# Sorting each partition's keys with 61 alternate-block stages at 30 falling distances in place of 69 stages of pruned odd-even merges

## The chip, the cores and the metric

The kernel runs on one core of a Trainium2 chip. The metric is the device time of one execution in microseconds (us). Before the change it was measured three times: 2129.62, 2132.74 and 2145.99 us; the median is 2132.74 us.

The engines are called as the profile calls them: PE is TensorE, DVE is VectorE, ACT is ScalarE, POOL is GpSimd and SP is SyncE, which issues most DMAs. Each engine works through its own queue of instructions in order; semaphores hold an instruction until what it reads or overwrites is ready.

## The reference

A GraphSAGE layer with mean aggregation: for each of 800,000 edges the row of the source node is added to the row of the destination node, the sums are scaled, and two 64x64 products are added.

```
N, deg, D = 12500, 64, 64
E = N * deg
def reference(x, src, dst, deg_inv, w_self, w_neigh):
    N = x.shape[0]
    # mean-aggregate neighbor features onto each destination node
    nsum = _segment_sum(x[src], dst, N)
    h_neigh = nsum * deg_inv[:, None]
    # GraphSAGE: W * CONCAT(h_v, AGG(h_u)) == W_self h_v + W_neigh h_N(v)
    return x @ w_self + h_neigh @ w_neigh
```

`src` and `dst` are drawn at random, `x` is 12,500 x 64 in 32-bit floats.

## The kernel before

The kernel sorts the edges by buckets of 144 destinations by 128 sources, so that gather and scatter become matrix products with one-hot matrices. It has these steps, one behind the other:

- **Keys** (`make_keys`, L405 to L414). The 800,000 edges lie as 128 partitions of 6,250. ACT and DVE make one 32-bit key of each edge, in seven pieces of columns, into buffer `a`.
- **Sorting each partition** (`sort_runs`, L221). Every partition's 6,250 keys are sorted along the columns by compare-exchange stages, all partitions at once. A stage reads one of the buffers `a` and `b` and writes the other. For a distance `dist` and a set `v` of columns, `emit` writes the minimum of columns `i` and `i + dist` to `i`, and the maximum to `i + dist`: two DVE instructions for each group of regular spacing (L232). Columns that a stage doesn't compare, but that the next one needs in the other buffer, are copied by ACT (L235). `spans` turns a set of columns into runs of equal length and spacing, so that one instruction takes many runs; `128x390x8` below is 390 runs of 8 columns.
- **Preparation** (`prepare`, `self_terms`, L515 to L599). It has nothing to do with the keys: `x` is split into two 16-bit floats and the product with `w_self` is made. The scheduler lays it beside the first stages of the sort. It has six ACT operations over 128x6272 elements (L538, L563, L565, L568, L573, L574), two such on DVE (L540, L564), and 26 small ACT copies from and to PE (L592, L597).
- **Finding rows** (`find_rows`, L443 to L466). ACT (L454) and DVE (L456) count, for each of 256 buckets of rows, how many keys lie below a bound in a window of the sorted columns. PE turns the counts, and POOL gathers runs of keys by them (L473).
- **Merging, decoding and sums.** DVE merges the gathered runs (L284, L296, L313, L328), the keys are decoded, and then PE multiplies one-hot matrices with `x` and sums into destinations (L827, L883), with ACT and DVE beside it.

The sort before is an odd-even merge sort. Thirteen levels merge ever finer interleaved sequences, and each level has a first stage at half its spacing and then stages at falling odd multiples; ranges that random keys hardly reach are pruned. That makes 69 stages, on average 3,012 compared pairs each. All spacings are powers of two. Where a level begins, ACT copies its untouched columns in one go (`alone`, `again`).

The last level is cut in two at column 2,560 (`SPLIT`): `below` runs all its stages for the low columns, then `above` for the rest, and the counts of the first 54 buckets (`EARLY`), which lie in the low columns, are laid on ACT beside `above`. `after_sort` writes this order out by hand, and everything from there to the end of the kernel; the stages ahead of it are placed by the scheduler, together with the preparation.

At the very end the kernel counts the edges that it found, and runs `general`, a slow loop over all edges, if the count isn't 800,000.

Of the kernel before, what the change touches and what calls it, by code (L numbers as in the profile page):

```python
# [17 lines left out]
AF = mybir.ActivationFunctionType  # L18
# [34 lines left out]
EARLY = 54  # L53
SHARED = 100
SPLIT = 2560
SIGMA = 6.0
LOWER = 2240
CLOSE = 32
# [92 lines left out]
def view(t, off, dims):  # L151
    a = t[:, :]
    dims = [d for d in dims if d[1] != 1] or [[1, 1]]
    return bass.AP(tensor=a.tensor, offset=a.offset + off, ap=[a.ap[0]] + dims)


def reach(k, n, total=None):

    i = np.arange(max(n - k, 0))
    m = 2.0 * i + k + 1
    var = m * (total - m) / total if total else m
    i = i[(k + 1.0) ** 2 <= SIGMA ** 2 * var]
    return (int(i[0]), int(i[-1]) + 1) if len(i) else (0, 0)


def distances(n, total=None):

    out = []  # L170
    k = 1
    while k < n:
        lo, hi = reach(k, n, total)
        if hi > lo:
            out.insert(0, (k, lo if lo > 3 else 0, hi))
        k *= 2
    return out


def spans(at):  # L180

    if not len(at):
        return []
    cut = np.flatnonzero(np.diff(at) != 1)
    out = []
    for lo, hi in zip(at[np.r_[0, cut + 1]].tolist(), (at[np.r_[cut, len(at) - 1]] + 1).tolist()):
        s = out[-1] if out else None
        if s and s[2] == hi - lo and (s[1] == 1 or lo - (s[0] + (s[1] - 1) * s[3]) == s[3]):
            if s[1] == 1:
                s[3] = lo - s[0]  # L190
            s[1] += 1
        else:
            out.append([lo, 1, hi - lo, 0])
    return out


def sort_levels(n):

    out = []
    R = 1
    while R < n:
        R *= 2
    at = np.arange(n)
    while R > 1:
        h = R // 2
        stages = [(h, at[(at % R < h) & (at + h < n)])]
        for k, lo, hi in distances(-(-n // R), -(-n // h)):
            i = at // R  # L210
            stages.append((k * R - h, at[(at % R >= h) & (i >= lo) & (i < hi) & (at + k * R - h < n)]))
        sets = [set(v.tolist()) | set((v + d).tolist()) for d, v in stages]
        assert all(x <= y for x, y in zip(sets[1:], sets[2:]))
        alone = sorted(set(range(n)) - sets[0])
        again = sorted(sets[0] - sets[1]) if len(sets) > 1 else []
        out.append((stages, np.array(alone, int), np.array(again, int)))
        R = h
    return out


def sort_runs(nc, bufs, n):  # L221

    levels = sort_levels(n)
    cur, oth = bufs

    def emit(src, dst, dist, v, low, cut, alone, again):
        for op, sh in ((OP.min, 0), (OP.max, dist)):
            for lo, g, l, st in spans(v[(v + sh >= low) & (v + sh < cut)]):  # L230
                x, y = (view(src, lo + o, [[st, g], [1, l]]) for o in (0, dist))
                nc.vector.tensor_tensor(view(dst, lo + sh, [[st, g], [1, l]]), x, y, op=op)  # L232
        for at, x, y in ((alone, src, dst), (again, dst, src)):
            for lo, g, l, st in spans(at[(at >= low) & (at < cut)]):
                nc.scalar.activation(view(y, lo, [[st, g], [1, l]]), view(x, lo, [[st, g], [1, l]]), AF.Copy)  # L235

    none = np.array([], int)
    for stages, alone, again in levels[:-1]:
        for j, (dist, v) in enumerate(stages):
            emit(cur, oth, dist, v, 0, n, *((none, none) if j else (alone, again)))  # L240
            cur, oth = oth, cur
    below, above = [], []
    stages, alone, again = levels[-1]
    edge = [SPLIT]
    for (first, _), (then, _) in zip(stages[-2::-1], stages[:0:-1]):
        edge.insert(0, edge[0] + max(first, then))
    assert edge[0] < n and not ((again > SPLIT) & (again < edge[0])).any()
    for j, (dist, v) in enumerate(stages):
        for l, low, cut in ((below, 0, edge[j]), (above, edge[j], n)):
            l.append(lambda a=(cur, oth, dist, v, low, cut, *((none, none) if j else (alone, again))): emit(*a))  # L250
        cur, oth = oth, cur
    return cur, below, above

# [86 lines left out]
class Kernel:  # L340
# [75 lines left out]
    def sort_edges(self, mps):  # L416

        nc, tc = self.nc, self.tc
        self.l1b = ExitStack()
        self.l1 = l1 = self.l1b.enter_context(tc.tile_pool(name="l1", bufs=1, side="right"))  # L420
        b = l1.tile([128, PITCH1], F32, name="b")
        self.c1 = l1.tile([128, 3, NC1], F32, name="c1")
        self.prow = l1.tile([128, 128], F32, name="prow")
        nc.gpsimd.iota(self.prow, pattern=[[PITCH1, 128]], base=0, channel_multiplier=0,
                       allow_small_or_imprecise_dtypes=True)
        self.l1ab = ExitStack()
        a = self.l1ab.enter_context(tc.tile_pool(name="l1a", bufs=1, side="right")).tile([128, PITCH1], F32, name="a")
        for t in (a, b):
            nc.gpsimd.memset(t[:, RUN:], BIG)
        with tc.tile_pool(name="raw", bufs=1) as raw:  # L430
            with tc.manual_schedule():
                self.make_keys(raw, a)
                nc.sync.dma_start(self.c1, self.I["c1"])
                for p in range(2):
                    nc.sync.dma_start(self.c2[p], self.I[f"c2_{p}"])
        self.runs, self.below, self.above = sort_runs(nc, (a, b), RUN)
        assert self.runs is b
        with tc.tile_pool(name="xp", bufs=1) as xp:
            self.prepare(xp, mps)
            self.self_terms(xp, mps)  # L440
        self.start = []
# [596 lines left out]
    def after_sort(self, es, mps, aps):  # L1038
# [5 lines left out]
        with tc.manual_schedule():  # L1044
            for step in self.below:
                step()
            tc.nc.sync.dma_start(self.d1[:, :SPLIT], self.runs[:, :SPLIT])
            rows = self.find_rows(0, mps)
            for i, step in enumerate(self.above):
                step()  # L1050
                while next(rows) + 1 < EARLY * (i + 1) // len(self.above):
                    pass
            tc.nc.sync.dma_start(self.d1[:, SPLIT:], self.runs[:, SPLIT:])
            self.l1ab.close()
# [125 lines left out]
```

## Time and profile before

| | |
|---|---|
| three runs | 2129.62, 2132.74, 2145.99 us |
| span of the profiled execution | 2141.8 us |
| DVE busy | 1998.3 us, 93% of the span |
| PE busy | 1022.8 us, 48% |
| ACT busy | 1260.8 us, 59% |
| keys begun, first sort stage begun | 3.63 us, 42.54 us |
| last sort stage ended | 512.46 us |
| first gather on POOL | 534.77 us |

The page of the profile gives the span alone for the profiled execution; it lies inside the range of the three runs and 9.1 us above their median. Up to 512 us the kernel is nearly one engine's work: DVE compares, ACT and PE work on the preparation in the first part, and POOL waits. From there to about 1,100 us DVE merges with POOL's gathers beside it. The rest, 1,042 us, is the matrix work, in which PE, ACT and DVE are all busy.

### The profile page before, as it was taken

The page shows a single profiled execution, that of the slowest core. Times are in us where ns is not written, and L with a number is a line of the kernel's source. Part 1 is how long each engine was busy: PE and PEld are TensorE (multiplying, and loading weights), DVE is VectorE, ACT ScalarE, POOL GpSimd, SP SyncE. Part 2 cuts the span into 40 slices and gives each one's busy share as a digit, 9 for nine tenths or more (in the row PEclk, how much of TensorE's full clock was granted, in tenths as well). Part 3 has the DMA queues.
Part 4 walks back from the last instruction along what each step waited for, and adds up shares of the span by engine and source line. Part 5 has one row for each costly group of instructions (what it writes and reads, how often), then busy time and mean ns, then how long its engine had stood idle before and what let it go on. Part 6 is the DMA issues. An engine that isn't in the chain of part 4 may idle for free.

```text
span 2141.8 us, 59532 instructions
## 1 busy us (share of the span) xinstructions
PE 1022.8 (48%) x26057; PEld 885.4 (41%) x26057; DVE 1998.3 (93%) x2172; ACT 1260.8 (59%) x1744; POOL 593.8 (28%) x867
## 2 busy tenths in 40 slices
PE   0140000000000000000299999999987799999997
PEld 0130000000000000000188788787876687888886
DVE  8999999999899999999999999999999988898887
ACT  7470000009700000162399999999998788888886
POOL 1000000000889888879810100000143000000000
PEclk9995555555555555555599999999999899999999
DMA  6040000000010000012477777777886677877874
GB/s 191 14 111 0 0 0 0 0 24 37 21 23 20 19 15 12 13 58 70 150 263 279 279 280 270 272 281 269 285 295 243 222 283 284 296 289 275 280 297 157
DMA packets 108220, 330.78 MB, mean 154 GB/s; under 512 B 53680, under 2 KB 61824, under 8 KB 107440
## 3 DMA queue, kind: packets, MB, share of 16 engines
q1 hardware_dynamic: 90784, 306.65, 39.4%
q0 software_dynamic: 14352, 18.65, 4.1%
q8 instruction: 205, 3.36, 0.6%
q10 hardware_dynamic: 2816, 1.61, 0.3%
q14 instruction: 63, 0.52, 0.1%
HBM read 307.86 MB, written 18.99 MB: 153 GB/s over the span
## 4 chain that ended last, share of the span: by engine, by line
PE 36%; DVE 30%; POOL 19%; issue 8%; ACT 5%; DMA 2%; ACTq 0%; DVEq 0%; POOLq 0%; SPq 0%
PE ct L827 21%; PE acc L883 14%; POOL u L473 13%; DVE a L232 10%; DVE b L232 10%; POOL pad L384 3%; ACT xg L837 2%; DVE ohd L802 2%; POOL v L633 2%; DVE ohs L799 2%; PE po L951 1%; DVE xg L835 1%; ACT junk L610 1%; DVE u L296 1%; ACT junka L454 1%
## 5 line engine op out<-in xcount | busy, mean ns | idle before, releaser
L837 ACT ACTIVATE xg<-ct 128x1024 f16<-128x1024 f32 (+1 forms) x991 | 934.8, 1105 | 102.2 <-PE ct L827 83.7
L827 PE MATMUL ct<-xh,ohs 128*128 128x128 f16 x8526 | 606.8, 223 | 47.7 <-issue 19.9
L827 PEld LDWEIGHTS <-ohs 128*128 128x128 f16 x8526 | 501.9, 99 | 91.7 <-issue 38.0
L473 POOL DMA_INDIRECT u<-d,ix x256 | 327.6, 1280 | 532.6 <-ACT junka L454 491.3
L296 DVE TENSOR_TENSOR u<-u 128x256 f32<-128x256 f32 (+47 forms) x494 | 452.6, 947 | 22.4 <-ACT u L280 15.3
L883 PE MATMUL acc<-ohd,xg 64*128 64x72 f16 x17052 | 413.0, 195 | 49.5 <-issue 27.1
L799 DVE TENSOR_SCALAR ohs<-slb,pidx 128x3584 f16<-128x3584 bf16 x305 | 351.0, 1151 | 32.8 <-PE ct L827 28.4
L883 PEld LDWEIGHTS <-xg 64*128 64x128 f16 x17052 | 327.1, 95 | 128.2 <-issue 47.4
L802 DVE TENSOR_TENSOR ohd<-iota,dlT 128x2016 f16<-128x2016 bf16 x305 | 366.7, 1202 | 0.0
L700 PE MATMUL tr<-idb,l 128*128 128x128 bf16 x68 | 9.1, 275 | 464.2 <-ACT l L694 460.6
L232 DVE TENSOR_TENSOR a<-b 128x106 f32<-128x106 f32 (+31 forms) x114 | 228.6, 2058 | 1.3
L232 DVE TENSOR_TENSOR b<-a 128x106 f32<-128x106 f32 (+36 forms) x112 | 227.4, 2081 | 1.0
L280 ACT ACTIVATE u<-u 128x256 f32<-128x256 f32 (+15 forms) x94 | 47.4, 595 | 281.6 <-DVE u L284 281.6
L463 PE MATMUL stp<-idf,st 128*128 128x128 f32 x2 | 0.9, 446 | 422.3 <-DVE st L461 422.3
L700 PEld LDWEIGHTS <-l 128*128 128x128 bf16 x68 | 5.5, 117 | 467.5 <-ACT l L694 464.0
L959 POOL DMA_DIRECT2D out<-o x24 | 22.8, 952 | 574.2 <-DVE o L958 491.2
L463 PEld LDWEIGHTS stp<-idf,st 128*128 128x128 f32 x2 | 0.4, 182 | 422.7 <-issue 422.7
L235 ACT ACTIVATE a<-b 128x106 f32<-128x106 f32 (+12 forms) x20 | 13.5, 709 | 214.1 <-DVE b L232 207.6
L835 DVE CAST xg<-ct 128x1024 f16<-128x1024 f32 x78 | 95.2, 1222 | 43.3 <-PE ct L827 43.2
L864 POOL DMA_INDIRECT lx<-xt,lxi x28 | 52.5, 1876 | 292.2 <-DVE lxi L862 165.9
L633 POOL DMA_INDIRECT v<-d,ix x68 | 89.9, 1323 | 63.5 <-ACT ix L663 44.6
L235 ACT ACTIVATE b<-a 128x1024 f32<-128x1024 f32 (+19 forms) x32 | 23.0, 771 | 130.4 <-DVE a L232 130.2
(135 smaller groups left out, 888.4 us busy)
## 6 DMA issues: line engine op xcount, KB each, us to landing
slb<-sl SPq DMA_DIRECT2D x305, 896.0 KB
u<-d,ix POOLq DMA_INDIRECT x256, 2.5
xt<-xh SPq DMA_DIRECT2D x1, 3136.0 KB
own<-os SPq DMA_DIRECT2D x12, 256.0 KB
fo<-own SPq DMA_DIRECT2D x24, 126.0 KB
out<-o POOLq DMA_DIRECT2D x24, 126.0 KB, 4.3
rd<-dst SPq DMA_DIRECT2D x4, 521.0 KB
rs<-src SPq DMA_DIRECT2D x4, 521.0 KB
```

The lines of the kernel that those rows point to most:

```text
L232: nc.vector.tensor_tensor(view(dst, lo + sh, [[st, g], [1, l]]), x, y, op=op)
L296: nc.vector.tensor_tensor(to, at(cur, ln + lo, n), at(cur, lo + k, n), op=op)
L384: self.nc.gpsimd.memset(self.pad, 0.0)
L473: nc.gpsimd.indirect_dma_start(out=u[:nr, p * w:(p + 1) * w], out_offset=None, in_=src, in_offset=bass.IndirectOffsetOnAxis(ap=self.start[ ...
L633: self.nc.gpsimd.indirect_dma_start(out=self.v[:, k].bitcast(F32), out_offset=None, in_=flat(self.d2[part], 128 * PITCH2[part]), in_offset ...
L799: nc.vector.tensor_scalar(s.rearrange("p c s -> p (c s)"), b, self.pidx[:, :1], None, op0=OP.is_equal)
L802: nc.vector.tensor_tensor(d, self.iota[:, None].to_broadcast([128, 14, HN, 2]), ix, op=OP.is_equal)
L827: nc.tensor.matmul(ct[:, i * 128:(i + 1) * 128], cols[i][0], self.xh[:, (b0 + i) % NB].rearrange("p a f -> p (a f)"), start=True, stop=True)
L835: nc.vector.tensor_copy(xg[:, :cnt * 128], ct[:, :cnt * 128])
L837: nc.scalar.activation(xg[:, :cnt * 128], ct[:, :cnt * 128], AF.Copy)
L864: nc.gpsimd.indirect_dma_start(out=x, out_offset=None, in_=self.xt, in_offset=bass.IndirectOffsetOnAxis(ap=ix.bitcast(U32), axis=0))
L883: nc.tensor.matmul(acc[h][:, db % OCT * HN:(db % OCT + 1) * HN], xg[r, i * 128:(i + 1) * 128], d[r], start=db % OCT == 0 and sb == 0, stop ...
```

## The change

The levels are replaced by a table of 61 stages, `GAPS`, of a distance and 0 or 1. At distance `g` the columns are cut into blocks of `g`; a stage with 0 compares block 0 with 1, 2 with 3 and so on, and a stage with 1 compares block 1 with 2, 3 with 4. There are 30 distances, from 2,568 down to 1, each used twice, and distance 1 a third time. A stage compares 2,944 pairs on average. What a stage leaves out at either end of the columns (`np.setdiff1d`) is copied by ACT in every stage. The last ten stages (`APART`, distances 5 to 1) are cut in two at column 2,560 as the last level was.

```diff
+APART = 10
+GAPS = ((2568, 0), (2568, 1), (1957, 0), (1957, 1), (1542, 0), (1542, 1), (1136, 0), (1136, 1), (867, 0), (867, 1), (659, 0), (659, 1), (509, 1), (509, 0), (393, 1), (393, 0), (319, 0), (319, 1), (245, 0), (245, 1), (186, 0), (186, 1), (145, 0), (145, 1), (114, 0), (114, 1), (88, 0), (88, 1), (68, 0), (68, 1), (53, 0), (53, 1), (41, 0), (41, 1), (31, 0), (31, 1), (24, 0), (24, 1), (18, 0), (18, 1), (14, 0), (14, 1), (11, 0), (11, 1), (9, 0), (9, 1), (7, 0), (7, 1), (6, 0), (6, 1), (5, 0), (5, 1), (4, 0), (4, 1), (3, 0), (3, 1), (2, 0), (2, 1), (1, 0), (1, 1), (1, 0))
...
-def sort_levels(n):
+def sort_stages(n):
...
+    every = np.arange(n)
+    for gap, odd in GAPS:
+        v = every[:n - gap]
+        v = v[v // gap % 2 == odd]
+        out.append((gap, v, np.setdiff1d(every, np.r_[v, v + gap])))
     return out
...
-        for at, x, y in ((alone, src, dst), (again, dst, src)):
-            for lo, g, l, st in spans(at[(at >= low) & (at < cut)]):
-                nc.scalar.activation(view(y, lo, [[st, g], [1, l]]), view(x, lo, [[st, g], [1, l]]), AF.Copy)
-
-    none = np.array([], int)
-    for stages, alone, again in levels[:-1]:
-        for j, (dist, v) in enumerate(stages):
-            emit(cur, oth, dist, v, 0, n, *((none, none) if j else (alone, again)))
-            cur, oth = oth, cur
+        for lo, g, l, st in spans(alone[(alone >= low) & (alone < cut)]):
+            nc.scalar.activation(view(dst, lo, [[st, g], [1, l]]), view(src, lo, [[st, g], [1, l]]), AF.Copy)
+
+    for dist, v, alone in stages[:-APART]:
+        emit(cur, oth, dist, v, 0, n, alone)
+        cur, oth = oth, cur
     below, above = [], []
-    stages, alone, again = levels[-1]
+    stages = stages[-APART:]
...
-    for j, (dist, v) in enumerate(stages):
+    for j, (dist, v, alone) in enumerate(stages):
         for l, low, cut in ((below, 0, edge[j]), (above, edge[j], n)):
-            l.append(lambda a=(cur, oth, dist, v, low, cut, *((none, none) if j else (alone, again))): emit(*a))
+            l.append(lambda a=(cur, oth, dist, v, low, cut, alone): emit(*a))
```

Counted from the two lists of stages: before, 226 DVE instructions with 415,716 columns (minima and maxima together) and 52 ACT copies with 34,300 columns; after, 198 DVE instructions with 359,200 columns and 87 ACT copies with 22,050. Behind the sort, the instructions of every engine are the same and stand in the same order; the lines of `kernel.py` behind the diff move up by 12.

Three places show how the instructions move. In the rows, `x2` at the end means two such instructions in a row, and the names are those of the tiles written and read.

The first place is DVE's queue where the last piece of keys is made and the sort begins (L410 to L414 make keys, L232 compares). Before:

```order
L410 SCALAR_TENSOR_TENSOR g<-h,rd 128x1040
L411 TENSOR_SCALAR a<-g 128x1040
L412 SCALAR_TENSOR_TENSOR g<-g,a 128x1040
L413 SCALAR_TENSOR_TENSOR s_226<-s_226,g 128x1040
L414 SCALAR_TENSOR_TENSOR a<-rs,s_226 128x1040
L232 TENSOR_TENSOR b<-a 128x2154 x2
L232 TENSOR_TENSOR a<-b 128x2048
```

The same place in DVE's queue after (L398 to L402 make keys, L223 compares):

```order
L398 SCALAR_TENSOR_TENSOR g<-h,rd 128x1040
L223 TENSOR_TENSOR b<-a 128x2568 x2
L399 TENSOR_SCALAR a<-g 128x1040
L400 SCALAR_TENSOR_TENSOR g<-g,a 128x1040
L401 SCALAR_TENSOR_TENSOR s_226<-s_226,g 128x1040
L402 SCALAR_TENSOR_TENSOR a<-rs,s_226 128x1040
L223 TENSOR_TENSOR a<-b 128x1114 x2
```

The first stage, which reads columns 0 to 5,135, now stands ahead of the last four key instructions, which make columns 5,210 to 6,249. The second stage stands right behind them, and reads columns 5,136 to 6,249 of `b`, which ACT copies.

The second place is ACT's queue in the preparation (L565 to L574 over 128x6272 elements, L592 and L597 small copies, L235 the sort's copies). Before:

```order
L565 ACTIVATE xh<-y 128x98x64
L592 ACTIVATE xs<-xt 128x512
L568 ACTIVATE y<-x,scl 128x6272
L597 ACTIVATE os<-pw 128x512
L592 ACTIVATE xs<-xt 128x512
L573 ACTIVATE z,s_530<-y 128x6272
L235 ACTIVATE a<-b 128x106
L597 ACTIVATE os<-pw 128x512
L592 ACTIVATE xs<-xt 128x512
L574 ACTIVATE z,s_531<-y,lim 128x6272
```

The same place in ACT's queue after (L553, L556, L561 and L562 are the four long operations, L225 the sort's copies):

```order
L553 ACTIVATE xh<-y 128x98x64
L585 ACTIVATE os<-pw 128x512
L580 ACTIVATE xs<-xt 128x512
L225 ACTIVATE a<-b 128x659
L556 ACTIVATE y<-x,scl 128x6272
L225 ACTIVATE b<-a 128x509
L585 ACTIVATE os<-pw 128x512
L225 ACTIVATE b<-a 128x367
L580 ACTIVATE xs<-xt 128x512
L225 ACTIVATE a<-b 128x142
L561 ACTIVATE z,s_517<-y 128x6272
L580 ACTIVATE xs<-xt 128x512
```

One copy of 106 columns stood among the four long operations; now the copies of stages 12, 13 and 14 stand between them (659; 509 and 367; 142 columns), and those of stage 15 (393 and 355) behind the fourth.

The third place is DVE's queue where short runs are compared. Before, at runs of 8:

```order
L232 TENSOR_TENSOR a<-b 128x390x8 x2
L232 TENSOR_TENSOR b<-a 128x247x8 x2
L232 TENSOR_TENSOR a<-b 128x359x8 x2
L232 TENSOR_TENSOR b<-a 128x375x8 x2
L232 TENSOR_TENSOR a<-b 128x383x8 x2
L232 TENSOR_TENSOR b<-a 128x387x8 x2
L232 TENSOR_TENSOR a<-b 128x389x8 x2
```

After, at distances 9 and 7:

```order
L223 TENSOR_TENSOR b<-a 128x347x9 x2
L223 TENSOR_TENSOR a<-b 128x346x9
L223 TENSOR_TENSOR a<-b 128x4
L223 TENSOR_TENSOR a<-b 128x346x9
L223 TENSOR_TENSOR a<-b 128x4
L223 TENSOR_TENSOR b<-a 128x446x7 x2
L223 TENSOR_TENSOR a<-b 128x445x7
L223 TENSOR_TENSOR a<-b 128x6
```

Eight stages at one spacing have become two, and runs of an odd length, every second of which begins at an odd column, take the place of runs of a power of two.

More of the change, by code (lines that the diff above doesn't have):

```diff
@@ L194, in spans, with emit @@
     return out
-def sort_levels(n):
+def sort_stages(n):
     out = []
[L202 to L217, printed above, removed]
+    every = np.arange(n)
[3 more added lines that the diff above has]
+        out.append((gap, v, np.setdiff1d(every, np.r_[v, v + gap])))
     return out
 def sort_runs(nc, bufs, n):
-    levels = sort_levels(n)
+    stages = sort_stages(n)
     cur, oth = bufs
-    def emit(src, dst, dist, v, low, cut, alone, again):
+    def emit(src, dst, dist, v, low, cut, alone):
         for op, sh in ((OP.min, 0), (OP.max, dist)):
@@ L232, in emit @@
                 nc.vector.tensor_tensor(view(dst, lo + sh, [[st, g], [1, l]]), x, y, op=op)
-        for at, x, y in ((alone, src, dst), (again, dst, src)):
-            for lo, g, l, st in spans(at[(at >= low) & (at < cut)]):
-                nc.scalar.activation(view(y, lo, [[st, g], [1, l]]), view(x, lo, [[st, g], [1, l]]), AF.Copy)
-    none = np.array([], int)
-    for stages, alone, again in levels[:-1]:
-        for j, (dist, v) in enumerate(stages):
-            emit(cur, oth, dist, v, 0, n, *((none, none) if j else (alone, again)))
-            cur, oth = oth, cur
+        for lo, g, l, st in spans(alone[(alone >= low) & (alone < cut)]):
[3 more added lines that the diff above has]
+        cur, oth = oth, cur
     below, above = [], []
-    stages, alone, again = levels[-1]
+    stages = stages[-APART:]
     edge = [SPLIT]
-    for (first, _), (then, _) in zip(stages[-2::-1], stages[:0:-1]):
+    for (first, *_), (then, *_) in zip(stages[-2::-1], stages[:0:-1]):
         edge.insert(0, edge[0] + max(first, then))
-    assert edge[0] < n and not ((again > SPLIT) & (again < edge[0])).any()
-    for j, (dist, v) in enumerate(stages):
+    assert edge[0] < n
+    for j, (dist, v, alone) in enumerate(stages):
         for l, low, cut in ((below, 0, edge[j]), (above, edge[j], n)):
-            l.append(lambda a=(cur, oth, dist, v, low, cut, *((none, none) if j else (alone, again))): emit(*a))
+            l.append(lambda a=(cur, oth, dist, v, low, cut, alone): emit(*a))
         cur, oth = oth, cur
```

## The prediction

> **What bounds the kernel now.** I read the page first: its span, the chain that ended last, and the groups of the sort.
>
> ```profile
> span 2141.8 us, 59532 instructions
> PE 36%; DVE 30%; POOL 19%; issue 8%; ACT 5%; DMA 2%; ACTq 0%; DVEq 0%; POOLq 0%; SPq 0%
> PE ct L827 21%; PE acc L883 14%; POOL u L473 13%; DVE a L232 10%; DVE b L232 10%; POOL pad L384 3%; ACT xg L837 2%; DVE ohd L802 2%; POOL v L633 2%; DVE ohs L799 2%; PE po L951 1%; DVE xg L835 1%; ACT junk L610 1%; DVE u L296 1%; ACT junka L454 1%
> L232 DVE TENSOR_TENSOR a<-b 128x106 f32<-128x106 f32 (+31 forms) x114 | 228.6, 2058 | 1.3
> L232 DVE TENSOR_TENSOR b<-a 128x106 f32<-128x106 f32 (+36 forms) x112 | 227.4, 2081 | 1.0
> L235 ACT ACTIVATE a<-b 128x106 f32<-128x106 f32 (+12 forms) x20 | 13.5, 709 | 214.1 <-DVE b L232 207.6
> L235 ACT ACTIVATE b<-a 128x1024 f32<-128x1024 f32 (+19 forms) x32 | 23.0, 771 | 130.4 <-DVE a L232 130.2
> ```
>
> The sort's compares (L232) are 226 instructions and 228.6 + 227.4 = 456.0 us of DVE, with 1.3 + 1.0 = 2.3 us of idle time before them, and 20% of the chain. ACT's copies (L235) take 36.5 us, and it is ACT that waits for DVE there.
>
> Next I took the busy time by stretches: the sort beside the preparation, the sort alone, and what follows. The columns are the stretch and its length, then each engine's busy time (count), PEclk, DMA share and GB/s.
>
> ```profile
> 42.54:160.00 117.46, 30.82 (x151) 25.96 (x151) 117.17 (x79) 65.88 (x56) 0.81 (x7) 0.97 0.33 83
> 160.00:512.40 352.40, 0.00 (x0) 0.00 (x0) 350.39 (x159) 43.27 (x143) 0.00 (x0) 0.50 0.01 4
> 512.40:2141.80 1629.40, 991.98 (x25906) 859.41 (x25906) 1495.96 (x1902) 1116.99 (x1509) 586.80 (x840) 0.81 0.54 192
> ```
>
> From 42.54 to 512.40 us DVE is busy in 467.6 of 469.9 us. The start of the sort's last pair, the first count behind it, and the waits show who follows:
>
> ```profile
> 508.39 4.07 DVE L232 TENSOR_TENSOR b<-a 128x1844 f32<-128x1844 f32 x2
> 512.38 0.41 DVE L456 TENSOR_SCALAR_CACHE_REDUCE junkd<-b,c 128x195 bf16<-128x195 f32 x1
> POOL u L473 <- ACT junka L454: 491.3, 1, 491.3
> ```
>
> The first count that DVE itself makes starts at the sort's end, and POOL's first gather waits 491.3 us in all, for ACT's counts, which need the sorted columns too. Nothing behind 512 us can begin before the sort ends, and nothing ahead of it is late but DVE. So a microsecond of DVE taken from the sort is a microsecond of the span.
>
> **Part 1: fewer and smaller stages.** The price of a compare comes from two pairs of different size in the timeline:
>
> ```profile
> 339.97 6.74 DVE L232 TENSOR_TENSOR a<-b 128x3124 f32<-128x3124 f32 x2
> 399.42 4.39 DVE L232 TENSOR_TENSOR b<-a 128x1996 f32<-128x1996 f32 x2
> ```
>
> A pair of 3,124 columns takes 6.74 us, one of 1,996 takes 4.39: (6.74 - 4.39) / 2 / 1,128 = 1.042 ns a column. The sort's 415,716 columns are then 433.0 us, and the other 23.0 of the 456.0 us, over 226 instructions, are 0.102 us each. After: 359,200 x 1.042 ns = 374.2 us, and 198 x 0.102 = 20.2 us, together 394.4. That is **61.6 us less**: 56,516 columns are 58.8 of it, 28 instructions 2.8. The gain lies on the chain, since DVE alone carries this stretch.
>
> **Part 2: copies in every stage.** ACT's own sum falls: 34,300 columns in 52 copies become 22,050 in 87. What matters is whether a stage must wait for one. A copy of a stage reads what the stage before wrote, runs beside its own stage, and is wanted by the next. So it has a whole stage, mostly over 5 us, as cover:
>
> ```profile
> 163.82 0.22 ACT L235 ACTIVATE a<-b 128x22 f32<-128x22 f32 x1 [9.40 <-DVE b L232]
> 163.82 6.85 DVE L232 TENSOR_TENSOR a<-b 128x3072 f32<-128x3072 f32 x4
> ```
>
> Here the 22 columns were copied in 0.22 us beside a stage of 6.85. From about 160 us ACT has nothing else to do and I cost these copies at nothing; if that cover went, it would be some 0.3 us at each of about 40 stages, 12 us. In the last ten stages ACT also has the 54 early counts, five or six to a stage. The first three, with the reading of each accumulator:
>
> ```profile
> 481.96 0.28 ACT L454 ACTIVATE junka<-b,c 128x2 bf16<-128x2 f32 x1
> 482.15 0.19 ACT L454 ACTIVATION_READ_ACCUMULATOR junka<-b,c 128x1 f32 x1
> 482.37 0.32 ACT L454 ACTIVATE junka<-b,c 128x32 bf16<-128x32 f32 x1
> ```
>
> 54 of them filled nearly all of the 30.5 us from 481.96 to the sort's end, so six are about 3.5 us. A stage of `above` now has 3,679 columns in 2.6 instructions on average (36,790 and 26 over ten), 4.1 us, and the tiny copy stands ahead of its group of counts; it is done a stage before it is wanted. Nothing again.
>
> Two places cost something. First, the second stage follows the last key instruction directly, and reads 1,114 columns that ACT can only copy once that instruction is done. ACT's price, and the four long operations for what follows:
>
> ```profile
> L235 ACT ACTIVATE b<-a 128x1024 f32<-128x1024 f32 x2 | 2.1, 1038 | 0.0
> 111.82 5.42 ACT L565 ACTIVATE xh<-y 128x6272 f16<-128x6272 f32 x1
> 117.14 0.59 ACT L592 ACTIVATE xs<-xt 128x512 f32<-128x512 f32 x1
> 117.62 5.52 ACT L568 ACTIVATE y<-x,scl 128x6272 f32<-128x6272 f32 x1
> 123.99 5.45 ACT L573 ACTIVATE z<-y 128x6272 bf16<-128x6272 f32 x1
> 130.54 5.55 ACT L574 ACTIVATE z<-y,lim 128x6272 bf16<-128x6272 f32 x1
> 104.28 6.73 DVE L564 SCALAR_TENSOR_TENSOR y<-x,scl,xh 128x6272 f32<-128x6272 f32 x1
> ```
>
> 1,024 columns take 1.04 us, so 1,114 about 1.1, and with the hand-over DVE stands **1.2 us**. Before, the first copy was made ahead of the keys' end.
>
> Second, the copies of stages 12 to 15 stand among the four long operations (the rows of ACT's queue above). I walk the two queues by hand. The first long one, 5.42 us, waits for DVE's 6.73 us operation, behind which DVE has the rest of stage 11 and stage 12, three compares of 2,636 columns at 2.85: 8.5 us. ACT needs up to 0.6 for a small copy it is in, 5.42, two more of 0.6, and 0.7 for 659 columns, with hand-overs and a PE wait of 1 us some 9.1: DVE waits 0.6. Then ACT needs 5.52, 0.6, 0.6 and 0.5 up to the copy of 367, 7.2 us, against stage 13's 6.0 (2 x 2.75 and 2 x 0.25): DVE waits 1.2. Then 5.45, 0.6, 5.55, the accumulators and the copy of 393, 12.9 us, run against stages 14 and 15, 12.5: 0.4. Together **2.2 us**. From below this is 0, if the small copies fall better; from above, every microsecond that ACT is late here is one of DVE's, and the last two operations, 11 us, are what can stand in front of one copy.
>
> **Part 3: runs of odd length.** Every compare of the sort before ran over runs of a power of two, or over every second column. Such a step of two words costs nothing extra: in the row below 1,285 columns at a step of two take 1.45 us, which is 1,285 x 1.042 ns + 0.11. The new stages at distances 11, 9, 7, 5, 3 and some longer ones have odd runs, of which every second begins at an odd word. Where the merge did that, and where DVE reads every sixth word:
>
> ```profile
> 469.28 2.90 DVE L232 TENSOR_TENSOR b<-a 128x1285 f32<-128x1285 f32 x2
> L296 DVE TENSOR_TENSOR u<-u 128x1728 f32<-128x1728 f32 x2 | 3.9, 1958 | 0.1
> L296 DVE TENSOR_TENSOR u<-u 128x1696 f32<-128x1696 f32 x2 | 3.8, 1919 | 0.0
> L745 DVE MAX8 top<-e 128x8 f32<-128x300 f32 x6 | 3.6, 666 | 0.0
> L745 DVE MAX8 top<-e 128x8 f32<-128x125 f32 x2 | 0.5, 284 | 0.0
> ```
>
> The 1,696 columns of L296 are 32 runs of 53, with one input beginning at an odd word (4097); the 1,728 are 32 runs of 54. 1,958 - 1,919 = 39 ns for 32 columns: the odd start costs nothing that shows. MAX8 at a step of six words takes (666 - 154) / 300 = 1.71 ns a word, 0.67 more than at a step of two (284 = 125 x 1.042 + 154). So a word that is fetched alone costs 0.67 ns, and one alone at the end of a long run nothing. The new sort has 12,142 odd runs over all its instructions: 0 by the first row, 8.1 us by the second. I take a quarter, **2 us**, since runs of 5 and more, nearer to the first row, are two thirds of them.
>
> [...]
>
> **The sum.** -61.6 + 1.2 + 2.2 + 2 = -56.2 us: a span of 2085.6 against 2141.8. The profiled execution lies 9.1 us above the median of the three runs; carried to that median, 2132.7 - 56.2 = **2076 us**.
>
> **The rivals.**
> - *ACT holds DVE in the preparation.* Were ACT late by the last two long operations and a few small copies, 11 us more, DVE would stand for it: 2088 us. For it: 65.9 us of ACT's work lie in that stretch and copies stand right behind 5 us operations. Against: my walk leaves gaps of a microsecond. Chance 0.13.
> - *Odd runs stall.* If the lone word of every run stalls once on the input side and once on the output side, 2 x 8.1 = 16 us in place of 2: 2090 us. For it, the MAX8 row; against it, the row of 53. [...] Chance 0.13.
> - *The gain is lost behind the sort*, in a wait that hangs on something else: 2133 us. The 491.3 us wait of POOL for the counts speaks against it. Chance 0.03.
> - *Every stage waits for its copies, and it gets slower.* The place is the border of each stage: all 65.9 us of ACT in the first stretch uncovered, and 0.5 us at each of 50 later borders, 25 us, make 90.9 - 61.6 = +29: 2162 us. It decides from 61.6 + 21 = 83 us of waits on. Before, 52 copies cost 2.3 us of idle time. With the case that the new network leaves keys out of place in some partition and the count at the end starts the loop over all edges (250 rounds of 25 columns with three gathers each, milliseconds): chance 0.05.
>
> **How the numbers follow.** The forecast has 0.66. The low end is no stall and no cost of odd runs, 2132.7 - 61.6 = 2071, less the 13 us by which the three runs lie above their median at most: 2058. The high end holds the two rivals at 2088 and 2090, and half of that scatter: 2098. Left out are the last two rivals, 0.08, and both at once. A measurement of this kernel tells about 1%, 21 us, from no change: the forecast and the first two rivals are faster by more, 0.92; the third is the same, 0.03; the fourth slower, 0.05.
>
> **What would show it.** The compares should sum to about 394 to 402 us in 198 instructions, the sort should end near 456 us, and the first gather come 56 us earlier, with a stretch behind the sort as long as before, 1,629 us. Part 2 is right if the idle time before the compares is near 3 us, in the waits at the second stage and at stages 13 to 16; wrong if waits for the copies add up to over 10. Part 3 shows in the pairs at 347x9 and 446x7 columns: 3.36 us a compare by 1.042 ns a column and 0.1, up to 4 with stalls. A stretch behind the sort that grew would make the prediction wrong.

## The result and the profile after

The changed kernel took 2080.40 us in the median of four runs (2070.78 to 2089.12); the kernel before, 2137.26 us over four (2129.62 to 2145.99). The ratio is 0.9735, with a 95% interval of 0.9693 to 0.9777: faster by 2.65%, 57 us. The forecast was 2076 us, 56.2 us below the 2132.7 us that it set out from. The granted clock, 0.774 in the profiled execution before and 0.987 in the one after, isn't the gain: the changed kernel took 2089.12 and 2080.30 us at 0.987, and 2080.50 and 2070.78 us at 0.77 to 0.78.

The page of the profile after: its span, the chain, and the groups of the sort (compares are L223 now, ACT's copies L225).

```profile
span 2087.4 us, 59594 instructions
PE ct L815 21%; PE acc L871 14%; POOL u L461 13%; DVE b L223 9%; DVE a L223 8%; POOL pad L372 3%; ACT xg L825 2%; POOL v L621 2%; DVE ohd L790 2%; DVE ohs L787 2%; DVE u L284 1%; PE po L939 1%; DVE xg L823 1%; DVE junkd L444 1%; ACT junk L598 1%
L223 DVE TENSOR_TENSOR b<-a 128x3120 f32<-128x3120 f32 (+38 forms) x106 | 205.8, 1993 | 3.2 <-ACT junka L442 0.5
L223 DVE TENSOR_TENSOR a<-b 128x3114 f32<-128x3114 f32 (+33 forms) x92 | 189.2, 2104 | 3.1 <-ACT b L225 2.0
```

The compares went from 456.0 us in 226 instructions to 205.8 + 189.2 = 395.0 in 198, and their part of the chain from 20% to 17%. The idle time before them rose from 2.3 to 6.3 us. The stretches of the changed kernel, cut at the sort's first compare, at 160 us, and at the sort's end:

```profile
37.71:160.00 122.29, 37.47 (x151) 31.69 (x151) 119.01 (x67) 67.00 (x64) 0.81 (x7) 1.00 0.31 78
160.00:456.40 296.40, 0.00 (x0) 0.00 (x0) 293.11 (x148) 41.00 (x176) 0.00 (x0) 1.00 0.01 5
456.40:2087.40 1631.00, 986.35 (x25906) 855.28 (x25906) 1495.18 (x1902) 1116.55 (x1505) 582.70 (x840) 0.98 0.54 192
```

The sort ends at 456.4 in place of 512.4 us, 56.0 earlier. What follows takes 1631.0 us, against 1629.4. The whole change of the span, 54.4 us, is the sort's 56.0 less 1.6 behind it. That the stretch behind the sort agrees within 1.6 us is partly luck: over the 13 kept traces, with all the experiments below, it lies between 1625 and 1642 us, and no run explains that scatter.

The end of the sort and the first gather, from the timeline:

```profile
452.38 4.07 DVE L223 TENSOR_TENSOR b<-a 128x1845 f32<-128x1845 f32 x2 [0.48 <-ACT junka L442]
478.12 1.03 POOL L461 DMA_INDIRECT u<-d,ix  x1 [429.28 <-DVE junkd L444]
```

The gather starts at 478.12 us in place of 534.77: 56.7 earlier, where the prediction asked for 56.

### The profile page after: what moved, and what is told of

It is laid out like the page before. It is cut to its first block, busy times and chain, and to the rows that moved or that the text cites. A ratio compares the mean times of both kernels' runs of the same rounds, so it can differ in the third digit from the quotient of the medians.

```text
span 2087.4 us, 59594 instructions
## 1 busy us (share of the span) xinstructions
PE 1023.8 (49%) x26057; PEld 887.0 (42%) x26057; DVE 1937.5 (93%) x2144; ACT 1257.6 (60%) x1779; POOL 589.7 (28%) x867
## 4 chain that ended last, share of the span: by engine, by line
PE 37%; DVE 28%; POOL 19%; issue 10%; ACT 5%; DMA 1%; DVEq 0%; ACTq 0%; POOLq 0%; SPq 0%
PE ct L815 21%; PE acc L871 14%; POOL u L461 13%; DVE b L223 9%; DVE a L223 8%; POOL pad L372 3%; ACT xg L825 2%; POOL v L621 2%; DVE ohd L790 2%; DVE ohs L787 2%; DVE u L284 1%; PE po L939 1%; DVE xg L823 1%; DVE junkd L444 1%; ACT junk L598 1%
## 5 line engine op out<-in xcount | busy, mean ns | idle before, releaser
L223 DVE TENSOR_TENSOR b<-a 128x3120 f32<-128x3120 f32 (+38 forms) x106 | 205.8, 1993 | 3.2 <-ACT junka L442 0.5
L223 DVE TENSOR_TENSOR a<-b 128x3114 f32<-128x3114 f32 (+33 forms) x92 | 189.2, 2104 | 3.1 <-ACT b L225 2.0
L225 ACT ACTIVATE a<-b 128x1 f32<-128x1 f32 (+44 forms) x57 | 22.2, 423 | 204.0 <-DVE b L223 201.4
L852 POOL DMA_INDIRECT lx<-xt,lxi x28 | 48.2, 1720 | 301.3 <-PE ct L815 165.8
L372 POOL MEMSET pad<- 128x89 f32 x457 | 90.3, 198 | 9.4
```

What stands on the lines that cost most here:

```text
L372: self.nc.gpsimd.memset(self.pad, 0.0)
L852: nc.gpsimd.indirect_dma_start(out=x, out_offset=None, in_=self.xt, in_offset=bass.IndirectOffsetOnAxis(ap=ix.bitcast(U32), axis=0))
```

## The experiments

Every experiment is an edit of the changed kernel. Ratios are to the kernel before, timed in the same rounds; the medians of that kernel differ between these timings (2137 to 2148 us). The experiments without a ratio were run once and are read by their traces, not by their times.

**Eight stages put back** (`e1_69`): are the stages the whole of the gain? Only the part of `GAPS` that changes is shown.

```diff
-(41, 0), (41, 1), (31, 0), (31, 1), (24, 0), (24, 1), (18, 0), (18, 1),
+(41, 0), (41, 1), (41, 0), (41, 1), (31, 0), (31, 1), (31, 0), (31, 1),
+(24, 0), (24, 1), (24, 0), (24, 1), (18, 0), (18, 1), (18, 0), (18, 1),
```

> Theory: the time follows the DVE columns of the sort, one for one. Eight stages put back (distances 41, 31, 24 and 18 twice as often) make 222 compares with 408,972 columns: 426.0 + 22.6 = 448.7 us of compares, 53.7 more than the 395.0 of the changed kernel; the sort ends near 510 us, the time is near 2134 us, no different from before (ratio 0.99 to 1.005). Rival: the gain came from something else that the change did, the first stage ahead of the last keys, the copies or a better start of what follows; then most of it stays, below 2110 us (ratio under 0.99).

Its groups of compares, and the timeline at the sort's end:

```profile
L223 DVE TENSOR_TENSOR b<-a 128x3100 f32<-128x3100 f32 (+38 forms) x118 | 232.9, 2026 | 3.0 <-ACT a L225 0.3
L223 DVE TENSOR_TENSOR a<-b 128x3075 f32<-128x3075 f32 (+33 forms) x104 | 216.3, 2128 | 3.3 <-ACT b L225 2.0
```

```profile
506.60 4.07 DVE L223 TENSOR_TENSOR b<-a 128x1845 f32<-128x1845 f32 x2
```

The compares sum to 449.2 us (448.7 expected), the sort ends at 510.67, and the ratio is 0.9996 (0.9964 to 1.0029): no different from before. 69 stages of the new kind cost about what 69 of the old kind did. The rival, a gain from something else in the change, falls.

**The first two stages swapped** (`e2_swap`): `GAPS` begins with (2568, 1), (2568, 0).

> Theory: the 1.2 us that DVE stands before the second stage is the copy of 1,114 columns that must follow the last keys. With the first two stages swapped, the first compares those columns itself and its copies are made earlier: that wait is gone, the others stay, and the sort ends about 1.2 us earlier, at 455.3 us. Rival: the wait only moves, to the next stage that ACT copies for (the two copies of 2,568 and 1,454 columns now come ahead), and the sort ends within 0.3 us of 456.5.

What the compares waited for, in the changed kernel and then with the swap (times in us, number of times):

```profile
L223 DVEq EVENT_SEMAPHORE  x51: 21/21/21, 56.3 to 451.9; - x51
its engine sat idle before it (us, times) until:
  ACT b L225: 2.0, 2
  ACT junka L442: 0.5, 1
  ACT a L225: 0.3, 1
```

```profile
L223 DVEq EVENT_SEMAPHORE  x51: 21/21/21, 55.6 to 450.3; - x51
its engine sat idle before it (us, times) until:
  ACT junka L442: 0.5, 1
```

The 1.2 us at the second stage are gone, and so are the 1.1 us later (0.3 at stage 13 and 0.85 at stage 14), which I hadn't expected. The sort's last pair begins at 450.76 and ends at 454.83, 1.6 us earlier than in the changed kernel. Only 0.7 of that is the swap's own: the third stage begins at 50.81 in place of 51.53 us. The rest comes from the later waits, and ACT's queue shows why they went. Its first long operation in the preparation, of the changed kernel and then with the swap:

```profile
114.06 5.42 ACT L553 ACTIVATE xh<-y 128x6272 f16<-128x6272 f32 x1
111.40 5.43 ACT L553 ACTIVATE xh<-y 128x6272 f16<-128x6272 f32 x1 [1.61 <-DVE y L552]
```

With the swap one pair of small copies fewer (one out of PE's result, one for its next) stands ahead of it, so it begins right behind DVE's operation on `y`.

**ACT made late** (`e5_actlate`): two more passes over `y` in the preparation.

```diff
         nc.scalar.activation(z, y, AF.Sign, bias=lim[:, :1], accum_out=s[1])
+        for _ in range(2):
+            nc.scalar.activation(z, y, AF.Sign)
```

> Two more passes of Sign over 128x6272 elements, 5.45 us each, are added to the preparation on ACT; nothing reads what they write. Rival of the prediction (ACT holds DVE): each microsecond that ACT is late is one of DVE's, so the waits for copies grow by 8 to 11 us and the sort ends near 466 us. Theory: a copy has a whole stage as cover and the scheduler puts copies between the long operations, so the waits grow by 1 to 2 us, and the sort ends near 458 us.

The waits with 11 us more work on ACT:

```profile
L223 DVEq EVENT_SEMAPHORE  x51: 21/21/21, 56.5 to 451.1; - x51
its engine sat idle before it (us, times) until:
  ACT b L225: 1.2, 1
  ACT junka L442: 0.5, 1
```

The waits didn't grow, they shrank by 1.1 us, and the sort ended at 455.65. The two passes stood at 139.36 and 145.96 us, with copies for the next stages right behind them, and no compare waited there: ACT's load isn't what holds DVE. The waits at stages 13 and 14 lie ahead of the two passes, so the passes can't have taken them away; why they went is seen on PE. Its rows at that place, of the changed kernel and then of this run:

```profile
106.87 2.07 PE L583 MATMUL pw<-w2s,xs 128*128 128x128 f32 x8 [0.69 <-ACT xs L580]
108.74 1.06 PE L577 MATMUL xt<-idf,x 128*128 128x128 f32 x4
```

```profile
107.02 1.16 PE L585 MATMUL pw<-w2s,xs 128*128 128x128 f32 x8 [0.69 <-ACT xs L582]
108.01 0.60 PE L579 MATMUL xt<-idf,x 128*128 128x128 f32 x4
```

The same eight matmuls took 2.07 and 1.16 us. ACT stands in order behind PE's results (L585 in the changed kernel, L587 here, wait for `pw`), so with the slower PE its first long operation began at 114.06 us, and with the faster at 112.25, and the copy behind it came 1.8 us sooner. Other runs bear this out. `e9_halves` below has the changed kernel's own early stages and no added work, its PE took 1.16 us too, and neither wait is there; `e1_69`, `e3_lone`, `e4_oddpairs` and `e10_changed_again` have 2.07 us at that place and both waits. With one pair of small copies fewer ahead of the long operation, as in `e2_swap`, the waits are gone at 2.07 us as well. So what sets these waits is how long ACT stands behind PE ahead of its first long operation, not the amount of ACT's work.

**All copies on DVE** (`e6_dvecopy`): what is ACT's part worth?

```diff
-            nc.scalar.activation(view(dst, lo, [[st, g], [1, l]]), view(src, lo, [[st, g], [1, l]]), AF.Copy)
+            nc.vector.tensor_copy(view(dst, lo, [[st, g], [1, l]]), view(src, lo, [[st, g], [1, l]]))
```

> All 87 copies of the stages go from ACT to DVE, so that no compare waits for another engine. Theory: the copies cost little where they were (2.8 us of waits, and 0.1 us for each of some 20 more semaphore instructions), so putting 22,050 columns in 87 instructions on DVE loses: at the 0.53 ns a column of the key's TENSOR_SCALAR 11.7 us, and 8.9 us of fixed cost, less 5 us of waits and gaps: the sort ends 15 us later, near 472 us. Rival: the copies held DVE by more than the gaps show, and the sort ends no later than 460 us.

Its groups on DVE up to the sort's end:

```profile
L223 DVE TENSOR_TENSOR b<-a 128x3120 f32<-128x3120 f32 (+41 forms) x106 | 205.9, 1992 | 0.7
L223 DVE TENSOR_TENSOR a<-b 128x2 f32<-128x2 f32 (+37 forms) x92 | 189.3, 2103 | 0.4
L225 DVE COPY a<-b 128x1 f32<-128x1 f32 (+44 forms) x57 | 15.4, 295 | 0.0
L225 DVE COPY b<-a 128x2 f32<-128x2 f32 (+21 forms) x30 | 8.2, 276 | 0.0
```

The copies take 15.4 + 8.2 = 23.6 us of DVE, and the sort ends at 470.11, 13.7 us later (15 expected). With no compare waiting for another engine, the idle time before the compares fell from 6.3 to 1.1 us, and the 51 semaphore instructions before compares are gone: this trace has none at that line. The stretches up to the sort's end close the sum:

```profile
37.91:160.00 122.09, 32.55 (x140) 27.81 (x140) 118.51 (x88) 45.17 (x33) 1.38 (x7) 0.89 0.30 75
160.00:470.11 310.11, 3.27 (x12) 2.39 (x11) 309.15 (x214) 35.86 (x135) 0.00 (x0) 0.50 0.02 6
```

DVE is busy 118.51 + 309.15 = 427.7 us, 15.5 more than the 412.1 of the changed kernel, and not 23.6 more: the records of the 87 copies overlap those beside them, by 0.09 us each on average (8.1 / 87; the copy at 465.86 us begins 0.08 before the compare ahead of it ends). The idle time before compares gives 5.2 us back, and a new wait of 3.1 us for ACT, ahead of a small DVE operation of the preparation (L563), takes most of that away again.

**Runs of three split into single words** (`e3_lone`): the price of a compare at a step of six words.

```diff
-                x, y = (view(src, lo + o, [[st, g], [1, l]]) for o in (0, dist))
-                nc.vector.tensor_tensor(view(dst, lo + sh, [[st, g], [1, l]]), x, y, op=op)
+                for j, k in ((j, 1) for j in range(l)) if dist == 3 else ((0, l),):
+                    x, y = (view(src, lo + j + o, [[st, g], [1, k]]) for o in (0, dist))
+                    nc.vector.tensor_tensor(view(dst, lo + j + sh, [[st, g], [1, k]]), x, y, op=op)
```

> Runs of 3 are split into three instructions over every sixth word, in the two stages at distance 3: 18 more compares, the same columns, some 430 columns each. Theory: words that are fetched alone cost a compare what they cost MAX8 at a step of six, 0.67 ns a column: 430 columns take 0.45 + 0.155 + 0.29 = 0.89 us, and the compares sum to 395.0 + 18 x 0.1 + 12,486 x 0.67 ns = 405 us. Rival: a compare, with two inputs and one output, streams any step at full rate, so 0.60 us each and a sum of 396.8 us.

The split instructions:

```profile
L224 DVE TENSOR_TENSOR a<-b 128x613 f32<-128x613 f32 x6 | 7.2, 1291 | 0.0
L224 DVE TENSOR_TENSOR b<-a 128x428 f32<-128x428 f32 x3 | 2.5, 909 | 0.0
```

428 columns took 0.909 us (0.89 expected, 0.60 by the rival): (909 - 155) / 428 = 1.76 ns a column. The 155 ns are what a compare at full rate took besides its columns (3,404 - 3,120 x 1.042 = 153 in `after`). The sort ended at 466.05 us, 9.6 later. So a step of six words cost a compare about what it cost MAX8: 1.76 ns a column here, 1.71 there.

**Pairs that begin on odd words** (`e4_oddpairs`): the blocks at distance 2 shifted by one column.

```diff
-        v = v[v // gap % 2 == odd]
+        o = int(gap == 2)
+        v = v[(v >= o) & ((v - o) // gap % 2 == odd)]
```

> In the two stages at distance 2 all blocks are shifted by one column, so that every run of two begins at an odd word; the compares have about 1,283 columns each and take 1.49 us in the changed kernel. Theory: an odd start is free as long as each 16 bytes give two words on average over the stream, which the distances 3 to 11 did; these pairs give 1.3 words to each 16 bytes, so they are slower: 1.9 to 2.4 us. Rival one: odd starts are free whatever the length: 1.49 us. [...]

The shifted compares of the first stage at distance 2 (641, 920 and 921 runs of two to an instruction):

```profile
L224 DVE TENSOR_TENSOR b<-a 128x1282 f32<-128x1282 f32 x2 | 3.0, 1492 | 0.0
L224 DVE TENSOR_TENSOR b<-a 128x1840 f32<-128x1840 f32 x1 | 2.1, 2077 | 0.0
L224 DVE TENSOR_TENSOR b<-a 128x1842 f32<-128x1842 f32 x1 | 2.1, 2072 | 0.0
```

All are at full rate, (1,492 - 155) / 1,282 = 1.04 ns a column, and my theory failed as I had applied it: I had counted 1.3 words to each 16 bytes, but at a pitch of four words, the second word of one such pair and the first of the next lie in the same 16 bytes, so each still holds two in a row. At this pitch the odd start cost nothing that shows; whether 16 bytes are the unit is not shown by this run.

**Halves of runs of four** (`e9_halves`): does it matter where a pair lies? Only the lines put in are shown.

```diff
+        o = int(gap == 4 and odd)
+        v = v[(v >= o) & ((v - o) // gap % 2 == odd)]
...
+                for j, k in ((0, 2), (2, 2)) if dist == l == 4 else ((0, l),):
+                    x, y = (view(src, lo + j + o, [[st, g], [1, k]]) for o in (0, dist))
+                    nc.vector.tensor_tensor(view(dst, lo + j + sh, [[st, g], [1, k]]), x, y, op=op)
```

> At distance 4 every run of four is split into two instructions, over its first and its second two words, at a pitch of eight words; in the second stage at that distance the blocks are shifted by one column. A half has about 642 or 917 columns, at full rate 0.82 or 1.11 us. Theory: the unit is 16 bytes, and a compare is slowed where fewer than two words come out of each; then the two halves of the first stage and the first half of the shifted stage (words 1 and 2) run at full rate, and the second half of the shifted stage (words 3 and 4, each in another 16 bytes) at 1.7 to 1.8 ns a column, 1.28 and 1.78 us. [...] Second rival: pairs are free wherever they begin, and all eight kinds run at full rate.

The groups of the unshifted stage (both halves), and then the four compares of the shifted stage one by one from the timeline, minimum of the first and second half, maximum of the first and second half:

```profile
L225 DVE TENSOR_TENSOR b<-a 128x646 f32<-128x646 f32 x2 | 1.6, 830 | 0.1
L225 DVE TENSOR_TENSOR b<-a 128x644 f32<-128x644 f32 x2 | 1.6, 824 | 0.0
```

```profile
390.17 0.83 DVE L225 TENSOR_TENSOR a<-b 128x642 f32<-128x642 f32 x1
390.91 1.32 DVE L225 TENSOR_TENSOR a<-b 128x642 f32<-128x642 f32 x1
392.20 0.83 DVE L225 TENSOR_TENSOR a<-b 128x642 f32<-128x642 f32 x1
392.94 1.29 DVE L225 TENSOR_TENSOR a<-b 128x642 f32<-128x642 f32 x1
```

The words are counted from 0 at the buffer's start. A first half (words 1 and 2 behind a multiple of four) ran at full rate, 0.83 us or 1.05 ns a column; a second half (words 3 and 4, which lie in two different 16 bytes) took 1.32 and 1.29, (1.30 - 0.155) / 642 = 1.78 ns a column. Both pairs begin on an odd word, so the odd start isn't what cost 0.7 ns here: the slow pairs are those with a border of 16 bytes, counted from the buffer's start, between their two words. That is the theory's outcome, shown for these pairs at a pitch of eight words.

**A version that goes further** (`e7_early72`, `e8_59`, `e10_changed_again`, `e11_59_again`). The first swaps two stages and raises `EARLY` from 54 to 72; the second has `EARLY` at 72 and leaves out (2568, 0) and (53, 1), which makes 59 stages; the last two time the changed kernel and the 59 stages on one chip.

> The first two stages swapped, and 72 early counts on ACT in place of 54. Theory: above now lasts 42 us against 31 before, and 54 counts fill 31 of it; ACT has 11 us free, 18 counts more. Behind the sort 56 counts are left of 74, so the first gather comes (74 - 56) / 74 x 21.7 = 5.3 us sooner after the sort's end, 16.4 us; with 1.2 us from the swap the time is 2074 us, ratio 0.970. Rival: ACT is not free, because its counts wait behind copies that wait for DVE; then the last stages wait for ACT by several us and the time stays at 2080.

> As with 72 early counts, and two stages fewer (2568 with 0, and 53 with 1). Theory: 59 stages, about 11,300 columns and 5 instructions fewer: 12 us off the sort, so about 2062 us, ratio 0.965. Rival: nothing more than noise beside the run with 61 stages.

> The changed kernel once more, on the same chip as the next: ratio to before 0.970 to 0.977.

> The version with 59 stages and 72 early counts again: its sort ended 13.1 us earlier than that of the changed kernel, and its first gather came 15.1 us earlier, so its time is 13 to 16 us below that of the changed kernel here, ratio to before 0.963 to 0.969. Rival: what follows gives it back, and the two are within 5 us.

With 72 early counts the first gather came at 474.15 us, 19.4 behind the sort's end in place of 21.7, not 16.4. The estimate had shrunk the work behind the sort evenly, but the 56 counts left are 26 on ACT and 30 on DVE, and ACT had one or two of the early ones to finish too. At some 0.6 us each ACT is through last, so DVE stood 2.48 us and POOL's wait ended with ACT's count, not DVE's:

```profile
471.68 0.29 DVE L448 TENSOR_TENSOR st<-acc,c 128x128 f32<-128x128 f32 x1 [2.48 <-ACT junka L442]
```

The ratio, 0.9735 (0.9680 to 0.9789), doesn't tell the 4 us of the trace from the changed kernel. The 59 stages have 11,284 columns and 4 instructions fewer; the sort ended at 443.39 us, the first gather came at 463.07, 15.1 us before the changed kernel's. Their ratios are 0.9622 (0.9567 to 0.9677) and, beside the changed kernel at 0.9745 (0.9707 to 0.9782), 0.9681 (0.9640 to 0.9723). Medians there are 2076.4 and 2084.9 us, 8.5 apart where 13 to 16 was expected. So it is ahead of the kernel before. That it is ahead of the changed kernel too is what its trace says, but not shown by these times: the two intervals overlap (0.9707 to 0.9723), and so do the single runs (2061.61 to 2086.40 against 2078.74 to 2093.85 us). Behind the sort its second trace took 1641 us (span 2084.7, sort's end 443.4) where its first took 1625: a scatter of 16 us that no run here explains. The granted clock, 0.783 and 0.990 in these two, doesn't: the first timing's four runs took 2070.29 and 2058.45 us at 0.99, and 2070.36 and 2060.59 us at 0.78.

## Why the prediction was right

The time, the direction and the mechanism came out: a microsecond of DVE taken from the sort was a microsecond of the span, and putting the stages back undid it. Of the sum's terms some were off, and that they cancelled in part is luck: the 5.4 us that were added for waits and odd runs met 4.3 us of idle time of another make-up.

- **Fewer and smaller stages.** -61.6 us was forecast, and the groups give 456.0 - 395.0 = -61.0. The groups of `a` and `b` overlap a little at their seams; by the stretches, DVE is busy 467.6 of 469.9 us before, and 412.1 of 418.7 after, of which 4.4 are the four key instructions that now stand behind the first stage. That is 407.7, so -59.9 of busy time and 6.6 - 2.3 = +4.3 idle: -55.6 against the 56.0 that the sort's end moved; the other 0.4 is an earlier start of the sort than the four key instructions account for.
- **The wait at the second stage.** 1.2 us forecast, 1.2 in the trace; `e2_swap` took it away, and 0.7 of it reached the third stage.
- **The waits at stages 13 to 16.** 2.2 us forecast, 0.3 at stage 13 and 0.85 at stage 14, none at 16. The queue walk named the place but not the cause. It let ACT's first long operation wait for DVE's operation on `y`; in the changed kernel that ended at 112.08 us, and ACT began at 114.06, held by small copies that stand behind PE. Where ACT did begin right behind DVE (`e2_swap`, `e5_actlate`, `e7_early72`, `e9_halves`), no compare of these stages waited, so the walk's own cause was worth nothing, and that half of its 2.2 us came all the same is luck. The rival that ACT's load would hold DVE fell: 11 us more work on ACT added no wait.
- **Copies from 160 us on at nothing.** This step was wrong in a small way: from 160 us on DVE's idle time is 296.40 - 293.11 = 3.3 us, against 352.40 - 350.39 = 2.0 before. ACT had the copies ready, but 51 compares have a semaphore instruction of 21 ns ahead of them, in place of the 13 of before (`L232 DVEq EVENT_SEMAPHORE  x13: 21/21/21, 52.0 to 484.3; - x13`). With the copies on DVE (`e6_dvecopy`) there is none. The idle time before all compares of the sort is 6.3 us, 2.8 of it in waits that the profile names; of the other 3.5, 2.4 go when the copies do (1.1 us idle in all in `e6_dvecopy`). Also, DVE stood 0.5 us before the last stage, which I had costed at nothing. The profile puts it to ACT's counts, but the one copy that this stage needs was done at 448.03 us, over 4 us before it began; five of the traces have that gap and six others with the new stages and ACT's copies don't, so its cause stays open.
- **Runs of odd length.** 2 us was taken between 0 and 8.1; it is next to nothing. The compares at distances 9 and 7 show it, beside a compare over runs of 24:

```profile
L223 DVE TENSOR_TENSOR b<-a 128x3123 f32<-128x3123 f32 x2 | 6.7, 3412 | 0.0
L223 DVE TENSOR_TENSOR b<-a 128x3122 f32<-128x3122 f32 x4 | 13.5, 3409 | 0.1
L223 DVE TENSOR_TENSOR b<-a 128x3120 f32<-128x3120 f32 x4 | 13.5, 3404 | 0.1
```

3,123 columns in runs of 9 took 3.412 us, 8 ns more than 3,120 in runs of 24; three columns more at full rate would be 3 ns, so next to nothing is left for the odd runs. The price of words one by one was right (`e3_lone`: 1.76 ns a column at a step of six), but these runs have two words or more in each 16 bytes on average; that a lone word at a run's end is made up for by its neighbours is my reading of it, which no run tests by itself. The rival of stalling odd runs falls.
- **The gain lost behind the sort, and the case that every stage waits.** Neither came: the stretch behind the sort is 1631.0 us against 1629.4, and DVE's idle time in the whole sort is 6.6 us against the 83 from which that case decides.

## What to carry to other kernels

Where one engine fills a stretch with 99% busy time and everything behind it waits for its end, price an edit by columns and instructions, and expect it one for one; then look for what the edit adds on the seams, because 28 fewer instructions saved 2.8 us here (by the forecast's price of 0.102 us each) and 38 more semaphore instructions, with four waits, gave 4.3 back. Copies handed to an idle engine were nearly free here, mostly with a whole stage between start and use: on DVE they added 15.5 us of busy time (`e6_dvecopy`), on ACT they cost DVE about 5 as waits and gaps (2.8 and 2.4).

## What the runs showed of the hardware

- A DVE compare in 32-bit floats ran at 1.04 ns a column and 155 ns besides in contiguous runs (2,568 columns in 2.824 us, `after`), every second word (1,845 in 2.078, `after`), runs of nine (3,123 in 3.412, `after`), runs of three (1,839 in 2.075, `after`) and pairs on odd words at a pitch of four (1,282 in 1.492, `e4_oddpairs`).
- It took 1.74 to 1.85 ns a column at a step of six words (`e3_lone`, means of the six groups of its 24 split compares), and 1.77 and 1.82 in pairs at a pitch of eight that lie in two different 16 bytes (`e9_halves`, 642 columns in 1.291 and 1.323 us). That a compare is slowed where each 16 bytes give it less than two words fits all of these; it is my reading of them.
- The same eight matmuls in the preparation took 2.07 us in one execution and 1.16 in another, at the same place in the program; the reason wasn't tried. A lower granted clock isn't it: it was 1.00 from 106 to 113 us in the trace with 2.07 (`after`); the 1.16 is from `e5_actlate`.
